# Recurrent-memory attention on one core: V on four column tiles with a bank of late values, Wo kept resident, another stage order

## The chip, the core and the metric

The kernel runs on one core of a Trainium2 chip. A core has TensorE (PE in the profile, with its weight loads as PEld), VectorE (DVE), ScalarE (ACT), GpSimd (POOL) and SyncE (SP, which here only issues transfers). TensorE reads SBUF and writes PSUM; VectorE and ScalarE copy PSUM back to SBUF. PSUM has eight banks, and part B below uses all of them. The metric is device time in microseconds of one execution; lower is better.

## The reference, cut to what matters

Two attentions run side by side and their outputs are concatenated. Part A is a sliding dilated attention, which this change leaves alone. Part B is a segment-recurrent attention with a memory of 8 rows: 64 segments of 32 tokens, model width 640, 32 heads of width 192.

```python
mem = mem0                                    # 8 rows
for s in range(n_seg):                        # 64 segments, in order
    h = jnp.concatenate([mem, xs], axis=1)    # 8 memory rows + 32 tokens = 40
    q = jnp.einsum('btd,dhe->bhte', h, Wq)    # k and v likewise
    scores = jnp.einsum('bhqe,bhke->bhqk', q, k) * scale
    scores = jnp.where(mask[None, None], scores, -1000000000.0)
    p = _softmax(scores, axis=-1)
    o = jnp.einsum('bhqk,bhke->bhqe', p, v)
    o = jnp.einsum('bhte,hed->btd', o, Wo)
    mem = o[:, :M, :].copy()                  # next segment needs this
    outs.append(o[:, M:, :])
```

The first 8 output rows of a segment are the memory of the next one, so the 64 segments form one chain. The four weight matrices of part B are 640 x 6144 each in bf16, too much to keep all of them in SBUF.

## The kernel before

**Order.** Resident weights are loaded first, then part A runs (16 blocks of 128 rows), then part B runs its 64 segments. The order of TensorE's instructions in part B is written out by hand in `segment`; the other engines' orders are laid out by the framework at build, each engine then works strictly in its own order. `evacuate` (line 267) sends PSUM copies to ScalarE and VectorE alternately.

**Rows and tokens.** A segment works on 40 rows: 32 that do not wait for the previous segment's result and 8 that do or nearly do. `HTs` holds the transposed rows in the order memory (8), then the tokens. For Q and K, the pass `project32` takes the first 32 of them (8 memory rows and 24 tokens) as 32-column weights on four column tiles of TensorE, five steps of four matmuls with 384 moving columns each (line 305). The remaining 8 tokens of a segment ("late" rows) are computed for four segments at a time: `XL` holds the late tokens of four segments, `project32` with `XL` fills the banks `Lq` and `Lk`, and GpSimd copies the 8 columns of the current segment from there (line 333). Each Q or K bank is renewed every four segments, so a segment has one doubled K pass and one late Q pass.

**A group of heads.** The 32 heads are worked in four groups of eight. For each group: a Q pass, a K pass, each copied to SBUF (`sb`, line 267) and turned by three matmuls against the identity (`turn`, line 318); the scores (line 368, 16 matmuls); a softmax on VectorE and ScalarE (lines 372 to 382); a V pass over all 40 rows (`values`, line 351, 64-column weights on two column tiles, 20 matmuls); P turned (`turn_p`, line 390, eight transposes); P times V (`mix`, line 404, 24 products over 40 keys in 64x64 tiles, two PSUM tiles, two copies); and the output projection (`project_out`, line 420, 24 matmuls per group) that accumulates into `Y`. At the segment's end `Y` is copied (`Ysb`, line 472), its memory rows are turned by six small matmuls (line 482) into the next `HTs`, and the output rows are stored by GpSimd's queue. `prep` (lines 275 to 284) loads and turns the next segment's tokens.

**Weights.** They are cut into pieces of 128 partitions: Q, K and V pieces of 384 KB and Wo pieces of 480 KB. All Q pieces are resident. `stream_plan` picks which of K, V and Wo are resident as well; the rest, 11 K, 9 V and 5 Wo pieces in each segment (704, 576 and 320 transfers in all), is streamed by SyncE's queue into five buffers at the place of use (`get_unit`, line 237). A buffer's next transfer is issued when TensorE has finished with the piece in it.

**PSUM.** Eight banks: three for the passes (`ps_acc`), two for turns (`ps_tr`), two for scores, turned P and P times V (`ps_at`), one for `Y`. Within a pool the buffers are taken in rotation, and an instruction that takes a buffer waits until the buffer's last reader is done.

Of the kernel before, what the change touches and what calls it, by code (L numbers as in the profile page):

```python
# [152 lines left out]
def stream_plan(budget):  # L153

    k = lambda g: [(("k", g, dc), 0.2) for dc in range(5)]  # L160
    v = lambda g: [(("v", g, dc), 0.35) for dc in range(5)]
    o = lambda g: [(("o", 4 * g + i, 0), 0.44) for i in range(4)]
    gap = lambda t: [(None, t)]
    steps = gap(1.0) + k(0) + gap(1.6) + k(1) + gap(0.8) + v(0) + gap(1.7) + k(2) + gap(0.6) + v(1)
    steps += gap(2.1) + k(3) + gap(0.6) + v(2) + gap(0.7) + o(0) + gap(1.0) + v(3) + gap(0.4)
    steps += o(1) + gap(0.7) + o(2) + o(3) + gap(1.9)
    size = lambda u: 3840 if u[0] == "o" else 3072
    total = sum(size(u) for u, _ in steps if u)
    span = sum(t for _, t in steps)
    for to_stream in range(total - budget, total, 64):  # L170
        now, done, streamed = 0.0, 0, []
        for u, t in steps:
            now += t
            if u is not None and done + size(u) / 2 <= min(5000 + to_stream * now / span, to_stream):
                streamed.append(u)
                done += size(u)
        if total - done <= budget:
            break
    return [u for u, _ in steps if u and u not in streamed]


def part_b(ctx, tc, B_x, B_mem0, B_Wq, B_Wk, B_Wv, B_Wo, out, ident, n_seg, budget, pre, nbuf, mid):
# [7 lines left out]
    wo_v = B_Wo.rearrange("h e d -> (h e) d").rearrange("(i p r) d -> p i (r d)", p=128, r=3)  # L190

    def unit_src(u):
        m, c, dc = u
        if m == "o":
            return wo_v[:, c, :]
        return w_in[m][:, dc, 1536 * c:1536 * c + 1536]
# [4 lines left out]
    resident = [("q", g, dc) for g in range(GROUPS) for dc in range(5)] + stream_plan(budget)  # L201
# [3 lines left out]
    def load_resident(pool, units):  # L205
        for k, u in enumerate(units):
            t = pool.tile([128, unit_cols(u)], BF16, name="wres_%s%d_%d" % u)
            res_engs[k % 2].dma_start(t[:], unit_src(u))
            res[u] = t[:]
# [12 lines left out]
    qk_sb = ctx.enter_context(tc.tile_pool(name="b_qk", bufs=3))  # L222
    one = ctx.enter_context(tc.tile_pool(name="b_one", bufs=1))
    small = ctx.enter_context(tc.tile_pool(name="b_small", bufs=4))
    ps_acc = ctx.enter_context(tc.tile_pool(name="b_ps_acc", bufs=3, space=PSUM))
    ps_tr = ctx.enter_context(tc.tile_pool(name="b_ps_tr", bufs=2, space=PSUM))
    ps_at = ctx.enter_context(tc.tile_pool(name="b_ps_at", bufs=2, space=PSUM))
# [4 lines left out]
    def get_unit(u):  # L232
        if u in res:
            return res[u]
        t = wstream.tile([128, 1920], BF16, tag="ws")
        v = t[:, 0:unit_cols(u)]
        nc.sync.dma_start(v, unit_src(u))
        return v
# [13 lines left out]
    Ps = [cpool.tile([128, 4 * L + PADW], BF16, name=f"P{i}") for i in range(2)]  # L252
# [5 lines left out]
    for t in HTs:  # L258
        nc.gpsimd.memset(t[:], 0.0)
    for t in QTs + Ps + OTs:  # L260
        nc.gpsimd.memset(t[:, t.shape[1] - PADW:], 0.0)
# [7 lines left out]
    def prep(s):  # L269
# [8 lines left out]
        pt = ps_tr.tile([128, 5, L], BF16, tag="tr")  # L278
# [7 lines left out]
    def prep_first():  # L286
# [5 lines left out]
        pt = ps_tr.tile([128, 5, L], BF16, tag="tr")  # L292
# [5 lines left out]
    def project32(Xs, m, g):  # L298

        ps = [ps_acc.tile([128, 384], FP32, tag="acc", name=f"pqk{n}") for n in range(len(Xs))]  # L300
        for dc in range(5):
# [6 lines left out]
        out = []  # L308
        for p in ps:
            sb = qk_sb.tile([128, 384], BF16, tag="sb", name="sb")  # L310
            evacuate(sb[:], p[:])
            out.append(sb)
        return out

    def turn(sb, dst):
        pt = ps_tr.tile([128, 3, 4, 32], FP32, tag="tr")
        for c in range(3):
            nc.tensor.matmul(pt[:, c], lhsT=sb[:, 128 * c:128 * c + 128], rhs=ident, start=True, stop=True)  # L318
        evacuate(dst.rearrange("p (j c) n -> p c j n", c=3), pt[:])
# [4 lines left out]
    def project_qk(s, m, g):  # L324
# [3 lines left out]
        sbs = project32([XL, HTs[s % 2]] if renew else [HTs[s % 2]], m, g)  # L328
# [9 lines left out]
    def project_late(m, g):  # L338
        sb = project32([XL], m, g)[0]
        return lambda: turn(sb, LT[m][g][:])  # L340

    def values(s, g):
        HT = HTs[s % 2]
        Vst = work.tile([128, 2, 384], BF16, tag="Vst")
        pv = [ps_acc.tile([128, 384], FP32, tag="acc", name=f"pv{c}") for c in range(2)]
        for dc in range(5):
            w = get_unit(("v", g, dc))
            for c in range(2):
                for gv in range(2):
                    n = 768 * c + 384 * gv  # L350
                    nc.tensor.matmul(pv[c][64 * gv:64 * gv + 64, :], lhsT=HT[:, dc, :], rhs=w[:, n:n + 384],  # L351
                                     start=(dc == 0), stop=(dc == 4), tile_position=(0, 64 * gv))
        for c in range(2):
            evacuate(Vst[:, c, :], pv[c][:])
        return Vst

    def scores(g):
        QT, KT = QTs[g % 2], tokens(KTs[g % 2])
        Sps = ps_at.tile([128, 4, L], FP32, tag="at")
# [7 lines left out]
        for n, (_, lo, a, g2, cc, hi) in enumerate(plist):  # L367
            nc.tensor.matmul(Sps[64 * g2:64 * g2 + 64, a, :], lhsT=QT[lo:hi, L * cc:L * cc + 64], rhs=KT[lo:hi, cc, :],  # L368
                             start=(g2 not in seen), stop=(n == last[g2]), tile_position=(lo, 64 * g2))
            seen.add(g2)  # L370
        t1 = work.tile([128, 4, L], FP32, tag="t1")
# [10 lines left out]
        nc.vector.tensor_tensor(out=Ps[g % 2][:, 0:4 * L].rearrange("p (a n) -> p a n", n=L), in0=t1[:],  # L382
                                in1=sm[:].unsqueeze(2).to_broadcast([128, 4, L]), op=ALU.mult)

    def turn_p(g):

        pt = ps_at.tile([128, 4, 128], BF16, tag="at")
        for a in range(4):
            for gv in range(2):
                nc.tensor.transpose(pt[64 * gv:64 * gv + 64, a, :], Ps[g % 2][:, L * a:L * a + 64], ident,  # L390
                                    tile_position=(0, 64 * gv))
        PT = work.tile([128, 4, 2, L], BF16, tag="PT")
        evacuate(PT[:], pt[:].rearrange("p a (h n) -> p a h n", h=2)[:, :, :, 0:L])
        return PT

    def mix(g, PT, Vst):

        ps = [ps_at.tile([128, 2, 3, L], FP32, tag="at", name=f"OTps{gv}") for gv in range(2)]
        V = Vst[:].rearrange("p c (h e r) -> p c h r e", h=2, r=3)
        for ai in range(2):  # L400
            for r in range(3):
                for half in range(2):
                    for gv in range(2):
                        nc.tensor.matmul(ps[gv][64 * half:64 * half + 64, ai, r, :],  # L404
                                         lhsT=V[64 * gv:64 * gv + L, ai, half, r, :],
                                         rhs=PT[64 * gv:64 * gv + L, 2 * ai + gv, half, :],
                                         start=True, stop=True, tile_position=(64 * gv, 64 * half))
        dst = OTs[g % 2][:, 0:12 * L].rearrange("p (ai gv n) -> p gv ai n", ai=2, gv=2)
        for gv in range(2):
            evacuate(dst[:, gv], ps[gv][:].rearrange("p a r n -> p a (r n)"))  # L410
# [13 lines left out]
    late = []  # L424

    def segment(s):
# [3 lines left out]
        while late:  # L430
            late.pop(0)()
# [6 lines left out]
        scores(0)  # L438
# [3 lines left out]
        scores(1)  # L442
        tk[2] = project_qk(s, "k", 2)
        tq[2]()
        PT[0] = turn_p(0)
        V[1] = values(s, 1)
        tk[2]()
        mix(0, PT[0], V[0])
        tq[3] = project_qk(s, "q", 3)
        scores(2)  # L450
        tk[3] = project_qk(s, "k", 3)
        tq[3]()
        PT[1] = turn_p(1)
        V[2] = values(s, 2)
        tk[3]()
        mix(1, PT[1], V[1])
        Y = ps_y.tile([128, 320], FP32, tag="y")
        project_out(Y, 0)
        scores(3)
        PT[2] = turn_p(2)  # L460
        if not last:
            prep(s + 1)
        V[3] = values(s, 3)
        mix(2, PT[2], V[2])
        project_out(Y, 1, range(0, 2))
        PT[3] = turn_p(3)
        project_out(Y, 1, range(2, 4))
        mix(3, PT[3], V[3])
        project_out(Y, 2)
        project_out(Y, 3)  # L470
        Ysb = work.tile([128, 320], BF16, tag="Ysb")
        nc.scalar.copy(Ysb[:], Y[:])
        if not last:
            late.append(project_late("q", (s + 1) % 4))
            HTn = HTs[(s + 1) % 2]
            pt = ps_tr.tile([128, 5, M], FP32, tag="tr")
            for dc in range(5):
                for gv in range(2):
                    c0, c1 = max(128 * dc, 320 * gv), min(128 * dc + 128, 320 * gv + 320)
                    if c0 < c1:  # L480
                        lo = c0 - 128 * dc
                        nc.tensor.matmul(pt[lo:lo + c1 - c0, dc, :], lhsT=Ysb[:, c0 - 320 * gv:c1 - 320 * gv],  # L482
                                         rhs=ident[:, 64 * gv:64 * gv + M], start=True, stop=True,
                                         tile_position=(0, lo))
            nc.vector.tensor_copy(HTn[:, :, 0:M], pt[:])  # L485
            late.pop(0)()
# [80 lines left out]
```

## Time and profile before

| | |
|---|---|
| median of 3 runs | 2506.86 us (2502.24 to 2510.97) |
| the profiled execution | 2491.66 us |
| its span | 2489.9 us |
| mean granted TensorE clock | 0.989 |
| first and last copy of Y (64 of them) | 364.0 and 2485.1 us |
| TensorE / VectorE / ScalarE / GpSimd busy | 89% / 49% / 30% / 12% |
| mean DMA rate over the span | 303 GB/s |

All times of the working come from the one profiled execution; it is 0.6% shorter than the median of the timed runs. The span consists of about 320 us of part A with the resident loads and then the 64 segments. In the profile, a row of a group gives line, engine, operation, output and inputs, the count, and the mean time of one instruction; a row in order of time gives start, duration and what ended the idle time before it. Matmuls overlap in TensorE's pipeline, so the durations of single matmuls are latencies, not their share of time: what a stage costs is read from the start of its first instruction to the start of the next stage's first.

### The profile page before, as it was taken

To read this page: it belongs to the slowest core of one execution; us is meant where nothing else is said; L and a number is where in the kernel's file an instruction comes from. 1 tells how busy PE (TensorE), PEld (TensorE's weight loads), DVE (VectorE), ACT (ScalarE), POOL (GpSimd) and SP (SyncE) were. 2 spreads that over 40 slices of the span, in tenths; PEclk is the share of its full clock that TensorE was granted. 3 is DMA by queue.
4 is the path that set the end of the run, shared out by engine and by line. 5 is a ranking of instruction groups with operands and counts; after the bars stand their busy time and mean duration, and the time that the engine had idled before them with its cause. 6 is when DMAs were issued, how large, how long until landed. Compare 5 with 4: busy or idle time off the path is not lost.

```text
span 2489.9 us, 92161 instructions
## 1 busy us (share of the span) xinstructions
PE 2206.2 (89%) x40618; PEld 1473.5 (59%) x40633; DVE 1214.1 (49%) x3110; ACT 749.6 (30%) x1811; POOL 287.7 (12%) x833
## 2 busy tenths in 40 slices
PE   0787679999999999999999999999999999999998
PEld 0455456666666666666665666666666666666665
DVE  1466534454444455444454444455444445444444
ACT  2122223333233333323333333333333333333332
POOL 1011111111111111111111111111011111111100
PEclk9899989999999999999999999999999999999999
DMA  7677689989888898888998899999888989889997
GB/s 294 214 259 255 220 315 320 319 306 311 309 312 315 309 316 307 303 313 303 312 316 298 310 313 311 313 319 318 304 314 315 308 313 312 311 313 316 318 320 270
DMA packets 279344, 754.65 MB, mean 303 GB/s; under 512 B 33192, under 2 KB 60656, under 8 KB 278944
## 3 DMA queue, kind: packets, MB, share of 16 engines
q1 hardware_dynamic: 260656, 705.44, 81.0%
q0 software_dynamic: 14208, 32.59, 4.2%
q10 hardware_dynamic: 4080, 10.73, 1.1%
q8 instruction: 318, 5.21, 0.8%
q14 instruction: 82, 0.67, 0.1%
HBM read 735.49 MB, written 13.15 MB: 301 GB/s over the span
## 4 chain that ended last, share of the span: by engine, by line
PE 48%; DMA 34%; DVE 4%; ACT 2%; issue 1%; ACTq 0%; POOL 0%; SPq 0%; POOLq 0%; DVEq 0%
DMA t<-in_B_Wo_dram 17%; PE pqk L305 16%; PE Y L420 11%; DMA t<-in_B_Wv_dram 10%; PE pv L351 9%; DMA t<-in_B_Wk_dram 6%; PE pt L318 4%; PE Sps L368 3%; PE pt L390 2%; PE OTps L404 2%; ACT sb L267 1%; ACT t L378 1%; DVE t L377 0%; DVE t L372 0%; DVE mx L376 0%
## 5 line engine op out<-in xcount | busy, mean ns | idle before, releaser
L420 PEld LDWEIGHTS <-OT 128*64 128x64 bf16 x6144 | 353.0, 110 | 110.4 <-issue 69.0
L351 PEld LDWEIGHTS <-HT 128*64 128x64 bf16 x5120 | 287.5, 110 | 148.8 <-issue 58.1
L420 PE MATMUL Y<-wres_o,OT 128*64 128x320 bf16 x4224 | 369.1, 301 | 0.0
L305 PEld LDWEIGHTS <-HT 128*32 128x32 bf16 x10240 | 242.5, 96 | 166.5 <-issue 43.2
L351 PE MATMUL pv<-t,HT 128*64 128x384 bf16 x2304 | 284.8, 329 | 40.1 <-DMA t<-in_B_Wv_dram 31.6
L351 PE MATMUL pv<-wres_v,HT 128*64 128x384 bf16 x2816 | 309.0, 328 | 0.2 <-DVE sb L267 0.2
L267 DVE CAST sb<-pqk 128x384 bf16<-128x384 f32 x324 | 180.3, 556 | 238.8 <-PE pqk L305 232.1
L305 PE MATMUL pqk<-wres_q,HT 128*32 128x384 bf16 x5120 | 258.7, 329 | 0.0
L267 ACT CAST sb<-pqk 128x384 bf16<-128x384 f32 x322 | 154.4, 479 | 334.0 <-PE pqk L305 333.3
L420 PE MATMUL Y<-t,OT 128*64 128x320 bf16 x1920 | 188.8, 302 | 54.1 <-DMA t<-in_B_Wo_dram 53.4
L305 PE MATMUL pqk<-t,HT 128*32 128x384 bf16 x2816 | 206.0, 329 | 28.1 <-DMA t<-in_B_Wk_dram 27.7
L318 PE MATMUL pt<-ident,sb 128*128 128x128 bf16 x1938 | 208.4, 222 | 11.6 <-ACT sb L267 11.6
L318 PEld LDWEIGHTS <-sb 128*128 128x128 bf16 x1938 | 109.8, 97 | 171.7 <-issue 111.0
L267 ACT CAST Vst<-pv 128x384 bf16<-128x384 f32 x256 | 122.7, 479 | 288.9 <-PE pv L351 288.2
L267 DVE CAST Vst<-pv 128x384 bf16<-128x384 f32 x256 | 141.5, 553 | 120.7 <-PE pv L351 120.2
L333 POOL COPY QT<-Lq 128x96 bf16<-128x96 bf16 x256 | 69.0, 269 | 917.0 <-PE Sps L368 816.8
L485 DVE CAST HT<-pt 128x40 bf16<-128x40 f32 x63 | 12.6, 200 | 312.3 <-PE pt L482 312.3
L372 DVE SCALAR_TENSOR_TENSOR t<-Sps,mask 128x160 f32<-128x160 f32 x256 | 83.0, 324 | 167.6 <-PE Sps L368 163.2
L305 PE MATMUL pqk<-wres_k,HT 128*32 128x384 bf16 x2304 | 160.4, 327 | 0.0
L368 PEld LDWEIGHTS <-QT 128*64 128x64 bf16 (+1 forms) x4096 | 114.9, 109 | 68.5 <-issue 46.8
L368 PE MATMUL Sps<-KT,QT 128*64 128x40 bf16 (+1 forms) x4096 | 139.0, 188 | 10.3 <-DVE KT L267 9.2
L378 ACT ACTIVATE t<-t 128x160 f32<-128x160 f32 x256 | 86.5, 338 | 203.5 <-DVE t L377 202.4
(93 smaller groups left out, 2570.8 us busy)
## 6 DMA issues: line engine op xcount, KB each, us to landing
t<-in_B_Wk_dram SPq DMA_DIRECT2D x704, 384.0 KB, 4.9
t<-in_B_Wv_dram SPq DMA_DIRECT2D x576, 384.0 KB, 5.1
t<-in_B_Wo_dram SPq DMA_DIRECT2D x320, 480.0 KB, 5.7
K<-a_kv_scr SPq DMA_DIRECT2D x16, 1280.0 KB, 6.2
V<-a_kv_scr POOLq DMA_DIRECT2D x16, 1280.0 KB, 8.8
a_kv_scr<-qkv POOLq DMA_DIRECT2D x16, 320.0 KB, 4.8
wres_q<-in_B_Wq_dram ACTq DMA_DIRECT2D x10, 384.0 KB, 7.8
wres_q<-in_B_Wq_dram SPq DMA_DIRECT2D x10, 384.0 KB, 7.8
```

What stands on the lines that cost most here:

```text
L267: (nc.scalar.copy if copies["n"] % 2 else nc.vector.tensor_copy)(dst, src)
L305: nc.tensor.matmul(ps[n][32 * j:32 * j + 32, :], lhsT=X[:, dc, 0:32], rhs=w[:, 384 * j:384 * j + 384], start=(dc == 0), stop=(dc == 4), ti ...
L318: nc.tensor.matmul(pt[:, c], lhsT=sb[:, 128 * c:128 * c + 128], rhs=ident, start=True, stop=True)
L333: nc.gpsimd.tensor_copy(tokens(T)[:, :, 32:L], LT[m][g][:, :, M * i:M * i + M])
L351: nc.tensor.matmul(pv[c][64 * gv:64 * gv + 64, :], lhsT=HT[:, dc, :], rhs=w[:, n:n + 384], start=(dc == 0), stop=(dc == 4), tile_position= ...
L368: nc.tensor.matmul(Sps[64 * g2:64 * g2 + 64, a, :], lhsT=QT[lo:hi, L * cc:L * cc + 64], rhs=KT[lo:hi, cc, :], start=(g2 not in seen), stop ...
L372: nc.vector.scalar_tensor_tensor(out=t1[:], in0=Sps[:], scalar=scale, in1=mask[:].unsqueeze(1).to_broadcast([128, 4, L]), op0=ALU.mult, op ...
L378: nc.scalar.activation(t1[:], t1[:], ACTF.Exp)
L390: nc.tensor.transpose(pt[64 * gv:64 * gv + 64, a, :], Ps[g % 2][:, L * a:L * a + 64], ident, tile_position=(0, 64 * gv))
L404: nc.tensor.matmul(ps[gv][64 * half:64 * half + 64, ai, r, :], lhsT=V[64 * gv:64 * gv + L, ai, half, r, :], rhs=PT[64 * gv:64 * gv + L, 2 ...
L420: nc.tensor.matmul(Y[64 * gv:64 * gv + 64, :], lhsT=OTs[g % 2][:, L * c:L * c + 64], rhs=w[:, n:n + 320], start=(i == 0 and r == 0), stop= ...
L485: nc.vector.tensor_copy(HTn[:, :, 0:M], pt[:])
```

## The change

The change touches part B alone.

- The V pass takes 32 rows on four column tiles, in the form of the Q and K passes (`project32`). The late rows' values are kept in new banks `LV`, one per group, renewed by a doubled pass (`XL` and `HT`) in one of four segments per group.
- P is written in two parts: 32 columns for the first keys, and 8 columns at the place of the current segment among the 32 late keys, in a tile of 64 columns whose other late columns are zero (GpSimd clears the previous segment's place for groups 0 and 1).
- P is turned by eight transposes with 32 output rows; P times V is a sum over the 32 keys of `Vst` and the 32 late keys of `LV`: 32 products per group, 16 with 128 columns and 16 with 64, on 32-row tiles, into four PSUM tiles with four copies.
- Wo is wholly resident, its rows in another order; 25 pieces of K and V, all of 384 KB, are streamed per segment from a fixed list, into six buffers.
- The two PSUM pools of two banks become one pool of four (`ps_x`). `qk_sb` has two buffers instead of three, `small` two instead of four, `Ysb` one instead of two.
- Stage order: P of a group is turned right after the next group's scores; each group's Wo follows the next group's V; `prep` stands behind the V pass of group 3; the late Q pass is split, three steps ahead of Wo of group 2 and two behind Wo of group 3; Wo of group 2 is split around the last turn and the last product.

```diff
+STREAMED = {"k": ((0, 1, 3, 4), (0, 2), (0, 1), (0, 1, 2, 3)),
+            "v": ((2, 4), (0, 1, 2, 4), (0, 1), (0, 1, 2, 3, 4))}
...
-    wo_v = B_Wo.rearrange("h e d -> (h e) d").rearrange("(i p r) d -> p i (r d)", p=128, r=3)
+    wo_v = B_Wo.rearrange("h e d -> (h e) d").rearrange("(i k p) d -> p i k d", p=128, k=3)
...
-    ps_tr = ctx.enter_context(tc.tile_pool(name="b_ps_tr", bufs=2, space=PSUM))
-    ps_at = ctx.enter_context(tc.tile_pool(name="b_ps_at", bufs=2, space=PSUM))
+    ps_x = ctx.enter_context(tc.tile_pool(name="b_ps_x", bufs=4, space=PSUM))
...
     def values(s, g):
+        renew = s == 0 or s % 4 == (g + 2) % 4
+        ps = project32([XL, HTs[s % 2]] if renew else [HTs[s % 2]], "v", g)
+        if renew:
+            evacuate(LV[g][:], ps[0][:])
+        Vst = work.tile([128, 384], BF16, tag="Vst")
+        evacuate(Vst[:], ps[-1][:])
         return Vst
...
+        i = s % 4
+        P = Ps[g % 2]
+        if g < 2 and s:
+            old = 32 + M * ((s - 1) % 4)
+            nc.gpsimd.memset(P[:, :, old:old + M], 0.0)
...
-        nc.vector.tensor_tensor(out=Ps[g % 2][:, 0:4 * L].rearrange("p (a n) -> p a n", n=L), in0=t1[:],
-                                in1=sm[:].unsqueeze(2).to_broadcast([128, 4, L]), op=ALU.mult)
+        for lo, hi, at in ((0, 32, 0), (32, L, 32 + M * i)):
+            nc.vector.tensor_tensor(out=P[:, :, at:at + hi - lo], in0=t1[:, :, lo:hi],
+                                    in1=sm[:].unsqueeze(2).to_broadcast([128, 4, hi - lo]), op=ALU.mult)
...
     def mix(g, PT, Vst):
+        ps = [ps_x.tile([128, 3, L], FP32, tag="x", name=f"OTps{a}") for a in range(4)]
+        for wide in (True, False):
+            for late, V in enumerate((Vst, LV[g])):
+                for half in range(2):
+                    for a in range(4):
+                        if wide:
+                            dst, e0, e1, col = ps[a][:, 2 * half, :], 256 * half, 256 * half + 128, 0
+                        else:
+                            dst, e0, e1 = ps[a][64 * half:64 * half + 64, 1, :], 128 + 64 * half, 192 + 64 * half
+                            col = 64 * half
+                        nc.tensor.matmul(dst, lhsT=V[32 * a:32 * a + 32, e0:e1], rhs=PT[32 * a:32 * a + 32, late, half, :],
+                                         start=(wide and late == 0 and half == 0), stop=(not wide and late == 1),
+                                         tile_position=(32 * a, col))
+        for a in range(4):
+            evacuate(OTs[g % 2][:, 3 * L * a:3 * L * a + 3 * L], ps[a][:].rearrange("p k n -> p (k n)"))
...
         tq[2] = project_qk(s, "q", 2)
-        scores(1)
+        scores(s, 1)
+        PT[0] = turn_p(0)
         tk[2] = project_qk(s, "k", 2)
         tq[2]()
-        PT[0] = turn_p(0)
+        mix(0, PT[0], V[0])
         V[1] = values(s, 1)
         tk[2]()
-        mix(0, PT[0], V[0])
+        Y = ps_y.tile([128, 320], FP32, tag="y")
+        project_out(Y, 0)
...
+        V[3] = values(s, 3)
         if not last:
             prep(s + 1)
-        V[3] = values(s, 3)
         mix(2, PT[2], V[2])
-        project_out(Y, 1, range(0, 2))
+        if not last:
+            gl = (s + 1) % 4
+            ql = project32([XL], "q", gl, range(0, 3))
+        project_out(Y, 2, range(0, 1))
         PT[3] = turn_p(3)
-        project_out(Y, 1, range(2, 4))
+        project_out(Y, 2, range(1, 3))
         mix(3, PT[3], V[3])
-        project_out(Y, 2)
+        project_out(Y, 2, range(3, 4))
         project_out(Y, 3)
```

## The prediction

> **What bounds the kernel now.** I read first the page's head and busy slices, then the waits, then one segment of part B in order of time, then the windows by stage.
>
> ```profile
> span 2489.9 us, 92161 instructions
> PE 2206.2 (89%) x40618; PEld 1473.5 (59%) x40633; DVE 1214.1 (49%) x3110; ACT 749.6 (30%) x1811; POOL 287.7 (12%) x833
> ...
> L472 ACT CAST Ysb<-Y x64: 426/426/428, 364.0 to 2485.1; 128x320 bf16<-128x320 f32 x64
> ...
> PE Y L420 <- DMA t<-in_B_Wo_dram: 53.4, 71, 2.4
> PE pv L351 <- DMA t<-in_B_Wv_dram: 31.6, 54, 1.1
> PE pqk L305 <- DMA t<-in_B_Wk_dram: 29.2, 51, 1.5
> ...
> 1500.00:1600.00 100.00, 94.02 (x1829) 62.86 (x1827) 49.16 (x138) 31.37 (x79) 11.96 (x36) 1.00 0.92 319
> ```
>
> TensorE is busy nine tenths of the span. One copy of Y ends each of the 64 segments: (2485.1 - 364.0)/63 = 33.67 us per segment is the unit of everything below. The three DMA waits sum to 114 us; with their companions on the weight loads I take 1.9 us per segment. The last row gives 319 GB/s at a DMA share of 0.92, so 347 GB/s would be full use. So the kernel is TensorE in program order, with the stream close behind.
>
> The stretches that carry the sum, TensorE rows first, then the softmax of group 3 and the copies beside it:
>
> ```profile
> 1008.46 1.00 PE L305 MATMUL pqk<-wres_q,HT 128*32 128x384 bf16 x20
> 1009.39 0.51 PE L318 MATMUL pt<-ident,sb 128*128 128x128 bf16 x6
> ...
> 1022.79 0.41 PE L390 MATMUL pt<-ident,P 128*64 128x128 bf16 x8
> 1023.03 0.49 PE L351 MATMUL pv<-wres_v,HT 128*64 128x384 bf16 x4
> ...
> 1024.76 0.34 PE L318 MATMUL pt<-ident,sb 128*128 128x128 bf16 x3
> 1025.03 0.45 PE L404 MATMUL OTps<-PT,Vst 40*64 40x40 bf16 x24
> 1025.41 0.60 PE L420 MATMUL Y<-wres_o,OT 128*64 128x320 bf16 x6
> ...
> 1027.07 0.52 PE L368 MATMUL Sps<-KT,QT 128*64 128x40 bf16 x16
> 1027.52 0.41 PE L390 MATMUL pt<-ident,P 128*64 128x128 bf16 x8
> 1027.64 0.33 DVE L372 SCALAR_TENSOR_TENSOR t<-Sps,mask 128x160 f32<-128x160 f32 x1 [1.60 <-PE Sps L368]
> 1027.87 0.29 PE L280 MATMUL pt<-ident,xr 40*128 40x40 bf16 x5
> 1028.30 0.30 ACT L281 COPY HT<-pt 128x160 bf16<-128x160 bf16 x1
> 1028.63 0.18 DVE L284 COPY XL<-pt 128x40 bf16<-128x40 bf16 x1
> 1029.71 0.32 DVE L382 TENSOR_TENSOR P<-t,sm 128x160 bf16<-128x160 f32 x1
> ```
>
> Matmuls overlap, so I cost TensorE by slots, start to next start. A Q or K pass: 1008.46 to 1009.39, 0.92 us. A V pass: 1023.03 to 1024.76, 1.73 us. Turning P: 0.24 us. P times V: 0.38 us. A softmax needs 1027.07 to 1030.03, 2.96 us from the start of its scores to P written.
>
> **The change, step by step, us per segment (minus is faster).**
>
> *V passes.* Twenty matmuls stay twenty, but on four column tiles instead of two, which is the form of the K pass: 1.73 becomes 0.92, four times: -3.27. The late rows' V is one more such pass inside a doubled one, 20 x 0.041 = +0.82 (the K pass with XL shows this step). All on the path.
>
> *P turned.* Eight transposes with 32 output rows for eight with 64: 0.24 to about 0.20, -0.2 over four groups.
>
> *P times V.* 24 products per group become 32: 16 with 128 columns, then 16 with 64. No row shows 32-row tiles. Lower bound: the old slot scaled, 0.38 x 32/24 = 0.51. Upper: the prep's five products (128-column weights, 40 moving) take 1027.87 to 1028.09, 44 ns each, 32 of them 1.41. I take 0.75: wide ones at the prep's inner pitch (first to last start, about 0.11 us over four steps, overlapped a little), narrow ones at the old 16 ns, and one extra change of tile form at about 0.1 (a pass followed by its like has a slot of 0.82, otherwise 0.92). Four times +0.37: +1.5. The Trainium skill, page "TensorEngine Tiling (Array Packing)", section Key Properties, says that changing the tiling mode drains the engine, which the 0.82 against 0.92 bears out, and it speaks against this mix; with four drains more and nothing else the sum would only move by +0.4.
>
> *Boundary.* Three of five steps of the late Q pass move ahead of Wo and stop covering the copy of Y. From the last Y matmuls (1003.25) to the next segment's first pass took 2.39; Now the memory rows start as soon as Y is copied (1004.32) instead of at 1004.71, which makes it 2.08, and the moved part costs 12 x 0.041 + 0.1 = 0.6 where it now stands: +0.3.
>
> TensorE work in sum: -0.9, bounds -1.9 and +1.8.
>
> *Stream.* 20 pieces of 384 KB and five of 480 KB become 25 of 384 KB: 10.32 to 9.83 MB, at 347 GB/s 29.7 to 28.3 us, with six buffers instead of five. Wo no longer waits. At 1.13 us a piece and six in hand, supply stays ahead of my walk until group 3's five V pieces in a row, where it is short by less than one. DMA waits 1.9 to 0.4: -1.5, bounds -1.9 and 0.
>
> *What is late next.* The two PSUM pools of two banks become one ring of four, and each P times V now takes all four. Its fourth product takes the bank of the turn (groups 0, 1) or of the prep (group 2) issued immediately before it, so TensorE, in order, stands until that copy is out, with the V pass, Wo and everything else queued behind.
> - Groups 0 and 1, at least: a turn's copy starts 0.43 after the turn, takes 0.48 (ScalarE) or 0.55, less the slot of 0.27: 0.7. In the built order the copy stands behind a softmax's exponential or its last write in part of the segments. Group 1: 0.75. Group 0, where the softmax of group 1 is fresh: 1.0.
> - Group 2: the XL copy of the prep, on VectorE, now stands behind the softmax of group 3, since prep moved behind the V pass. From the scores' start TensorE needs 0.48 + 0.20 + 0.92 + 0.22 = 1.82 (2.64 when V is doubled). VectorE needs 2.96, plus 0.2 for a second write of P, 0.2 for a copy of PT in front and 0.2 for XL: 3.6 (4.2 with a V copy between). Wait 1.65.
> - turn of P(0), now right after scores 1, and K of group 1: 0.35. The q3 turn behind the exponential of group 2 on ScalarE: 0.25. First Wo pair after the last mix, 0.15.
>
> Together 4.15. Before, such waits were 0.45 (KT, sb and XL behind VectorE and ScalarE). So +3.7; bounds +1.5 (1.2 instead of 3.4 before the mixes, rival 1) and +5.1 (groups 0 and 1 both at 1.6, behind the last write of P in every segment). The memsets on GpSimd (two per segment) and the token copies behind them are hidden: GpSimd is 12% busy and its longest queue waits for TensorE; without the cover they cost about 0.27 each. The same page, section PSUM Bottleneck, warns that after a fourfold tiling the copies out of PSUM may bind; VectorE at 49% busy would by that rule leave room on average, and it is the order that I charge.
>
> *One-off.* The first segment has four doubled V passes: +3. The Wo rows are read in runs of 1280 bytes instead of 3840, once, 16 pieces: hidden behind segment 0 or up to +10.
>
> **Sum.** -0.9 - 1.5 + 3.7 = +1.3 us per segment, times 63 = +83, plus 3: +86 us. The profiled execution took 2491.66 us (span 2489.9), 15 us under the median 2506.86 of the runs shown. On the median: **2593 us**.
>
> **Rivals.**
> 1. *Faster: the copies come in time.* ScalarE and VectorE lose three of eight V copies per segment (0.48 to 0.55 each), so the queues I see may be shorter, and three of four products start before the held one. With 1.2 us before the mixes instead of 3.4, the sum is -0.9 per segment, -55: 2452 us. It decides where the waits before the three mixes fall below 2.1 us per segment. For it: ScalarE is 30% busy. Against: the order is fixed at build and the softmax chain is longer than the V pass that now covers it.
> 2. *DMA waits stay.* If five V pieces in 0.8 us leave the 1.9 us of waits, +1.5 more: 2688 us. Against: Wo, the largest wait, is resident.
> 3. *P times V at its upper bound* 1.41: +2.6 more, 2759 us. Against: today's mix issues at 16 ns in 64x64 tiles.
> 4. *Nothing changes:* held only by the turn or prep right before (0.7, 0.7, 0.77), the sum is about +0.1: 2510 us.
>
> **How the numbers follow.** Main case 0.50 (own range 2540 to 2645), rival 1 0.24, rival 2 0.10, rival 3 0.10, rival 4 0.06. A change under about 0.3% can't be told from none here. Slower: 0.50 + 0.10 + 0.10 and a part of rival 4 = 0.72; same 0.04; faster 0.24. The range goes from rival 1's value to rival 2's, 2450 to 2690, and leaves out most of rival 3 and the far side of rival 1.
>
> **What would show it.** V slots of 0.92 and a Y period near 35 us; TensorE busy share below 89%; waits of the OTps products on VectorE and ScalarE copies of about 1.0, 0.75 and 1.65 us, the last on XL; DMA waits near 25 us in sum. I am wrong if the OTps products start straight after the turn, or if the mix slot lies far from 0.75.

## The result, and the profile after

The changed kernel takes 2654.60 us (median of 4 runs, 2628.65 to 2659.82) against 2504.55 us (2490.48 to 2510.97) for the kernel before on the same chip: a ratio of 1.0587, interval 1.0503 to 1.067. It is slower by 150 us, 64 more than forecast; the profiled executions, 2659.82 and 2491.66 us, are 168 us apart. In the order of the fences before the prediction:

From the page of the changed kernel (span, busy time, landing of the streamed pieces) and its tile view of Ysb:

```profile
span 2658.0 us, 99823 instructions
PE 2207.7 (83%) x44021; PEld 1331.0 (50%) x44021; DVE 1195.5 (45%) x3527; ACT 713.3 (27%) x1973; POOL 298.8 (11%) x959
...
t<-in_B_Wv_dram SPq DMA_DIRECT2D x832, 384.0 KB, 5.7
t<-in_B_Wk_dram SPq DMA_DIRECT2D x768, 384.0 KB, 5.5
...
L467 ACT CAST Ysb<-Y x64: 425/425/426, 376.3 to 2653.2; 128x320 bf16<-128x320 f32 x64
```

TensorE is busy for the same time as before (2206.2 us then), and the rest of the span has grown. The segment takes (2653.2 - 376.3)/63 = 36.14 us instead of 33.67: 2.47 x 63 = 156 us; the other 12 us lie before the first copy of Y (376.3 instead of 364.0), 3.7 of them in the first segment (44.1 instead of 40.4) and the rest ahead of it, where part B's first pass starts at 332.20 instead of 323.56.

The waits of TensorE in the changed kernel (us in total, times, longest us):

```profile
PE acc L289 <- DMA t<-in_B_Wv_dram: 143.0, 223, 2.2
...
PE OTps L388 <- ACT QT L250: 40.1, 81, 0.8
PE OTps L388 <- DVE XL L267: 36.9, 60, 1.3
PE OTps L388 <- DVE QT L250: 33.2, 46, 1.2
PE acc L289 <- DMA t<-in_B_Wk_dram: 30.2, 55, 1.1
```

The three rows of OTps are the forecast holds of the fourth product: 110 us. The two rows of DMA are not as forecast: 173 us where 25 were expected and where the kernel before had 114.

The timeline of TensorE in one segment of the changed kernel (start, us, operation, count, idle before and its releaser). In order of time: a mix that is held and a V pass; an undisturbed mix of group 3 with the Wo behind it; and, a segment later, the last V pass and the start of the Wo tail:

```profile
1405.39 0.19 PE L388 MATMUL OTps<-PT,Vst 32*128 32x40 bf16 x3
1406.03 0.20 PE L388 MATMUL OTps<-PT,Vst 32*128 32x40 bf16 x5 [0.44 <-ACT QT L250]
...
1406.40 0.71 PE L289 MATMUL acc<-t,HT 128*32 128x384 bf16 x8
...
1407.53 0.34 PE L302 MATMUL pt<-ident,sb 128*128 128x128 bf16 x3
...
1418.35 0.22 PE L388 MATMUL OTps<-PT,Vst 32*128 32x40 bf16 x8
...
1418.74 1.50 PE L402 MATMUL Y<-wres_o,OT 128*64 128x320 bf16 x18
...
1446.81 0.93 PE L289 MATMUL acc<-t,HT 128*32 128x384 bf16 x16
1449.56 0.35 PE L289 MATMUL acc<-t,HT 128*32 128x384 bf16 x4 [1.82 <-DMA t<-in_B_Wv_dram]
...
1451.92 1.01 PE L402 MATMUL Y<-wres_o,OT 128*64 128x320 bf16 x6
1452.86 0.40 PE L370 MATMUL pt<-ident,P 128*32 128x128 bf16 x8
```

Three products of a mix go and the fourth stands until the turn's copy is out (1405.39 to 1406.03). The mix of group 3, with no turn ahead of it, takes 1418.35 to 1418.74, 0.39 us for 32 products. The last V pass stands 1.82 us for its last piece. Six Wo matmuls then take 0.94 us (1451.92 to 1452.86); at the rate of group 0, 24 from 1407.81 to 1409.46, they would take 0.41.

Where the stream is meanwhile: the waits of SyncE's queue (total, times, longest), the DMAs that it issues over the end of this segment, and two windows of the same segment (us, busy time of the five engines, granted clock, DMA share, GB/s):

```profile
SPq L217 <- PE acc L289: 1542.9, 892, 11.4
```

```profile
1440.30 3.79 SPq L217 DMA_DIRECT2D t<-in_B_Wv_dram  x5
1444.19 6.08 SPq L217 DMA_DIRECT2D t<-in_B_Wk_dram  x6
1460.23 1.59 SPq L217 DMA_DIRECT2D t<-in_B_Wv_dram  x2
```

```profile
1426.40:1434.40 8.00, 6.84 (x160) 3.94 (x153) 5.50 (x18) 2.83 (x7) 0.74 (x3) 1.00 1.00 370
...
1454.40:1459.40 5.00, 4.83 (x97) 2.83 (x97) 0.87 (x4) 1.32 (x4) 0.97 (x2) 0.91 0.01 5
```

SyncE issues the next segment's six K pieces by 1450.3, and then nothing for ten microseconds, until TensorE has used the first of them (1459.85). Six pieces are all that six buffers hold. Such waits for a buffer last up to 11.4 us; before, the longest was 3.7. Once these six pieces have landed, the DMA engines do nothing (share 0.01 from 1454.40 to 1459.40); while pieces are being issued they are nearly full (0.91 from 1423.4 to 1450.4, and 1.00 with 370 GB/s in the window shown) and TensorE waits. Before, with five Wo pieces among the 25, five windows of 8 us in a row (1000 to 1040) had shares of 0.75 to 0.99.

Slots on TensorE, start to next start as in the prediction, summed from the traces over 63 segments (us per segment; a wait counts to the slot that it interrupts). The last column is the time between the first and the last copy of Y in which the record of the granted clock stands at one half. The two lower rows are the first two experiments, without streamed transfers:

| | period | Q, K, V passes | Wo | mixes | turning P | half-rate clock in part B, us in all |
|---|---|---|---|---|---|---|
| before | 33.67 | 17.75 | 7.88 | 1.56 | 1.10 | 10 |
| after | 36.14 | 18.04 | 8.12 | 3.94 | 0.70 | 263 |
| b_nostream | 31.22 | 16.47 | 6.78 | 1.53 | 1.06 | 0 |
| a_nostream | 31.50 | 13.95 | 7.13 | 4.54 | 0.61 | 20 |

### The profile page after: what moved, and what is told of

Same layout as the page of the kernel before. It is cut to its first block, busy times and chain, and to the rows that moved or that the text cites. A ratio compares the mean times of both kernels' runs of the same rounds, so it can differ in the third digit from the quotient of the medians.

```text
span 2658.0 us, 99823 instructions
## 1 busy us (share of the span) xinstructions
PE 2207.7 (83%) x44021; PEld 1331.0 (50%) x44021; DVE 1195.5 (45%) x3527; ACT 713.3 (27%) x1973; POOL 298.8 (11%) x959
## 4 chain that ended last, share of the span: by engine, by line
PE 45%; DMA 38%; DVE 7%; ACT 4%; issue 2%; SPq 0%; ACTq 0%; POOL 0%; POOLq 0%; DVEq 0%
DMA t<-in_B_Wv_dram 29%; PE acc L289 18%; PE Y L402 14%; DMA t<-in_B_Wk_dram 5%; PE OTps L388 4%; PE pt L302 3%; DMA K<-a_kv_scr 2%; PE Sps L342 1%; DVE sb L250 1%; DMA a_kv_scr<-qkv 1%; PE pq L65 1%; ACT QT L250 1%; DVE K L98 1%; PE pt L370 1%; ACT sb L250 1%
## 5 line engine op out<-in xcount | busy, mean ns | idle before, releaser
L289 PE MATMUL acc<-t,HT 128*32 128x384 bf16 x6400 | 475.8, 333 | 143.5 <-DMA t<-in_B_Wv_dram 114.4
L289 PEld LDWEIGHTS <-HT 128*32 128x32 bf16 x15360 | 383.8, 97 | 376.7 <-issue 213.9
L402 PE MATMUL Y<-wres_o,OT 128*64 128x320 bf16 x6144 | 552.1, 330 | 1.8 <-issue 1.4
L250 DVE CAST sb<-acc 128x384 bf16<-128x384 f32 x371 | 206.0, 555 | 267.2 <-PE acc L289 222.7
L289 PE MATMUL acc<-wres_q,HT 128*32 128x384 bf16 x5120 | 259.5, 330 | 0.2 <-ACT sb L250 0.2
L388 PE MATMUL OTps<-PT,Vst 32*128 32x40 bf16 (+1 forms) x4096 | 146.9, 197 | 112.8 <-ACT QT L250 40.1
L250 DVE CAST OT<-OTps 128x120 bf16<-128x120 f32 x512 | 121.0, 278 | 229.1 <-PE OTps L388 227.5
L250 ACT CAST sb<-acc 128x384 bf16<-128x384 f32 x275 | 130.8, 476 | 223.8 <-PE acc L289 162.8
L289 PE MATMUL acc<-t,XL 128*32 128x384 bf16 x1676 | 144.1, 337 | 34.7 <-DMA t<-in_B_Wv_dram 28.6
L289 PE MATMUL acc<-wres_k,HT 128*32 128x384 bf16 x2048 | 148.7, 327 | 1.0 <-issue 1.0
```

The lines of the kernel that those rows point to most:

```text
L250: (nc.scalar.copy if copies["n"] % 2 else nc.vector.tensor_copy)(dst, src)
L289: nc.tensor.matmul(ps[n][32 * j:32 * j + 32, :], lhsT=X[:, dc, 0:32], rhs=w[:, 384 * j:384 * j + 384], start=(dc == 0), stop=(dc == 4), ti ...
L388: nc.tensor.matmul(dst, lhsT=V[32 * a:32 * a + 32, e0:e1], rhs=PT[32 * a:32 * a + 32, late, half, :], start=(wide and late == 0 and half = ...
L402: nc.tensor.matmul(Y[64 * gv:64 * gv + 64, :], lhsT=OTs[g % 2][:, L * c:L * c + 64], rhs=w[:, n:n + 320], start=(i == 0 and r == 0), stop= ...
```

## The experiments

Theory S: the 25 pieces are now wanted in the first three quarters of the segment, and what TensorE loses, it loses to the stream. Theory B: the held products (the fourth of each mix) make the loss. Every run is timed against the kernel before on its own chip. That kernel took 2504.55 us on the chip of the result and 2495.41, 2498.12, 2496.99 and 2506.62 us on the four chips below, so a difference in us between runs of two chips is good to about 10 us. All medians:

| run | us | ratio to before |
|---|---|---|
| b_nostream | 2331.52 | 0.9333 [0.928, 0.9387] |
| a_nostream | 2360.38 | 0.9442 [0.9389, 0.9495] |
| a_order | 2599.08 | 1.0403 [1.0328, 1.0479] |
| a_spread | 2581.67 | 1.0343 [1.0272, 1.0414] |
| a_order_nostream | 2175.58 | 0.8711 [0.867, 0.8751] |
| a_both | 2496.28 | 1.0006 [0.9984, 1.0028] |
| a_plan | 2524.52 | 1.0107 [1.0042, 1.0172] |
| a_plan6 | 2367.69 | 0.9492 [0.9444, 0.954] |
| a_spread6 | 2441.10 | 0.9787 [0.9721, 0.9853] |
| b_buf6 | 2390.93 | 0.9571 [0.9512, 0.9629] |
| a_deep7 | 2511.82 | 1.0019 [0.9985, 1.0052] |
| a_deep12 | 2401.86 | 0.9593 [0.9557, 0.9628] |

### Both kernels without streamed transfers

The streamed piece is replaced by a resident one, in the kernel before (b_nostream, where a streamed Wo piece gives way to a resident one of Wo) and in the changed one (a_nostream); this is the edit of the latter:

```diff
-        t = wstream.tile([128, 1536], BF16, tag="ws")
-        nc.sync.dma_start(t[:], unit_src(u))
-        return t[:]
+        return res[("q", u[1], u[2])]
```

> The kernel before, without the streamed transfers: where a K, V or Wo piece would be streamed, a resident Q or Wo piece is read instead, so the output is not the reference's; all matmuls and copies stay. Both theories: the DMA waits of 1.9 us per segment go, 2504 becomes about 2385 us, and the half-rate clock stays rare (10 us before).

> The changed kernel, without the streamed transfers (a resident Q piece is read in place of each of the 25; the output is not the reference's). Theory S (stream: with Wo resident, all 25 pieces are asked for in the first 25 us of a segment, the transfers run full there and idle in the tail; DMA waits of 2.7 us and the half-rate clock behind them are the loss): DMA waits go, 173 us, and the clock recovers, about 95 us: about 2390 us. Theory B (banks: P times V held by the ring of four is the loss): the holds stay and grow from the measured 2.2 to the walked 3.4 us per segment, since nothing else gives the copies time: about 2560 us.

2331.52 and 2360.38 us. So the stream costs 2495 - 2332 = 164 us in the kernel before (2495.41 on this chip) and 2655 - 2360 = 294 us in the changed one (timed on another chip), and all else that the change does costs 29 us. That is S by the forecast. The table of slots shows the 29 us as a difference of larger things: passes 16.47 to 13.95 (-2.52 per segment), mixes 1.53 to 4.54 (+3.01), Wo +0.35, turning P -0.45. The mix slot of group 3 shows that the products themselves cost nothing more, so the +3.01 are holds. From the waits of TensorE in a_nostream:

```profile
PE OTps L386 <- DVE XL L265: 69.3, 60, 1.3
...
PE OTps L386 <- ACT QT L248: 43.5, 81, 0.8
PE OTps L386 <- DVE QT L248: 40.5, 46, 1.2
```

Without DMA waits the holds are longer (153 us against 110), nearly all of it at group 2 (69.3 against 36.9), whose mix stands right behind the V pass of group 3: a wait for a piece of that V gives the copy time to finish.

### The holds taken away, and the stream spread, each alone

a_order moves the mixes of groups 0 and 1 ahead of the turn that they waited for, and the prep ahead of V of group 3; that takes a third buffer for the copies of Q and K, paid for with the second buffer of one scratch tile (these two lines are not shown):

```diff
         tk[2] = project_qk(s, "k", 2)
-        tq[2]()
         mix(0, PT[0], V[0])
         V[1] = values(s, 1)
+        tq[2]()
         tk[2]()
...
-        V[3] = values(s, 3)
         if not last:
             prep(s + 1)
+        V[3] = values(s, 3)
         mix(2, PT[2], V[2])
```

a_spread puts back the old stream, with its five 480 KB buffers (11 pieces of K, 9 of V, 5 of Wo), and leaves the rest of the change:

```diff
-    resident += [(m, g, dc) for g in range(GROUPS) for m in "kv" for dc in range(5) if dc not in STREAMED[m][g]]
-    resident += [("o", i, 0) for i in range(4 * GROUPS)]
+    resident += stream_plan(103700)
...
-    part_b(ctx, tc, B_x, B_mem0, B_Wq, B_Wk, B_Wv, B_Wo, out, ident, n_seg=n_seg, pre=110000, nbuf=6,
+    part_b(ctx, tc, B_x, B_mem0, B_Wq, B_Wk, B_Wv, B_Wo, out, ident, n_seg=n_seg, pre=110000, nbuf=5,
```

> The changed kernel with the holds of P times V taken away by order alone: mix 0 and mix 1 stand before the Q turn instead of behind it, prep before the V pass of group 3; three sb buffers instead of two, t1 single. Theory B: 2.2 us per segment go, about 2515 us. Theory S: the time saved before pieces that are late turns into more DMA waits; only the hold of group 2, behind the last piece, is a gain, 0.9 us per segment: about 2600 us.

> The changed kernel with the stream of before: 11 K, 9 V and 5 Wo pieces in five buffers of 480 KB, the other 15 pieces' worth resident; stage order, banks and V on four tiles as changed. Theory S: demand reaches into the tail again, DMA waits fall from 173 to about 110 us and the clock recovers: about 2500 us. Theory B: holds stay, about 2620 us.

2599.08 and 2581.67 us: 55 and 73 below the changed kernel, neither near a full recovery. In a_order the holds were gone, and TensorE stood for V instead:

```profile
PE acc L289 <- DMA t<-in_B_Wv_dram: 221.1, 333, 3.1
...
PE acc L289 <- DMA t<-in_B_Wk_dram: 17.2, 41, 1.0
```

The DMA waits went from 173 to 238 us. What a hold had cost was mostly time in which the stream caught up. By its number (2600 expected) S is right, but B's cause is there as well, under it.

### The holds without a stream, and both cures together

a_order_nostream is a_order with the edit of a_nostream; a_both is a_order with the edit of a_spread.

> The changed kernel with the holds taken away by order (as in a_order) and without the streamed transfers (a resident Q piece is read instead; the output is not the reference's): what TensorE alone needs. In the changed kernel without transfers a segment took 31.50 us with P times V at 4.54; with P times V at 1.86, as a_order showed it, 28.8 us, 2360 - 170 = 2190 us if the holds are a cost of their own (both theories). If instead the time only moves to other waits of TensorE on the copies, 2280 us or more.

> The changed kernel with the order of a_order and the stream of before (a_spread): holds gone, demand reaching into the tail. Theory S: the two gains do not simply add (-55 and -73 from 2655 would be 2527), because without holds the pieces are wanted even earlier; but the transfers now have the whole segment: 10.3 MB at 347 GB/s is 29.7 us of a 28.8 us walk, so 2450 to 2530 us. Theory B: -2.2 us per segment below a_spread, 2440 us.

2175.58 us: without transfers the holds are worth 2360 - 2176 = 185 us (2.9 per segment), and the changed work without them is 156 us faster than b_nostream. With the old stream back the same order gave 2496.28 us, the time of the kernel before (ratio 1.0006): 85 us below a_spread, but 321 above its own twin without transfers. Without transfers this order saves 31.22 - 28.62 = 2.6 us per segment on the kernel before; with them, five buffers and its stream, it saves nothing (33.59 against 33.67): what TensorE gains it waits for.

### A list by the demand, then a sixth buffer

a_plan is a_both with the streamed pieces spread again by the new order of demand (12 K, 5 V, 8 Wo, 2.9% more bytes); a_plan6 has one buffer more. Its list has as many pieces of each kind, with one Wo piece exchanged for its neighbour:

```diff
-    v = lambda g: [(("v", g, dc), 0.35) for dc in range(5)]
-    o = lambda g: [(("o", 4 * g + i, 0), 0.44) for i in range(4)]
+    v = lambda g: [(("v", g, dc), 0.2) for dc in range(5)]
+    o = lambda a, b: [(("o", i, 0), 0.42) for i in range(a, b)]
...
-    steps = gap(1.0) + k(0) + gap(1.6) + k(1) + gap(0.8) + v(0) + gap(1.7) + k(2) + gap(0.6) + v(1)
-    steps += gap(2.1) + k(3) + gap(0.6) + v(2) + gap(0.7) + o(0) + gap(1.0) + v(3) + gap(0.4)
-    steps += o(1) + gap(0.7) + o(2) + o(3) + gap(1.9)
+    steps = gap(0.8) + k(0) + gap(1.3) + k(1) + gap(0.8) + v(0) + gap(1.7) + k(2) + gap(0.5) + v(1)
+    steps += gap(0.7) + o(0, 4) + gap(1.4) + k(3) + gap(0.5) + v(2) + gap(0.7) + o(4, 8) + gap(0.8) + v(3) + gap(1.1)
+    steps += o(8, 9) + gap(0.2) + o(9, 11) + gap(0.5) + o(11, 16) + gap(1.7)
...
-    resident += stream_plan(103700)
+    resident += stream_plan(102300)
...
-    part_b(ctx, tc, B_x, B_mem0, B_Wq, B_Wk, B_Wv, B_Wo, out, ident, n_seg=n_seg, pre=110000, nbuf=5,
+    part_b(ctx, tc, B_x, B_mem0, B_Wq, B_Wk, B_Wv, B_Wo, out, ident, n_seg=n_seg, pre=110000, nbuf=6,
```

> a_both with the list of streamed pieces laid out anew for this order, evenly over a segment by TensorE's measured stage times: 12 K, 5 V and 8 Wo pieces, five buffers of 480 KB. Theory S: with even demand DMA waits fall below those of before (1.9 us per segment) and the half-rate clock is rare: 2350 to 2420 us, faster than both kernels. Theory B: like a_both.

> a_plan with six buffers of 480 KB instead of five, nearly the same list. If a piece's time to land (5 to 6 us with the queue full) is what the waits come from, 20 to 60 us below a_plan; if the full rate of the transfers is, the same as a_plan.

Two misses. The list by demand made it no better (2524.52 us, 28 above a_both). The buffer, which I had put at 20 to 60 us, was worth 157: 2367.69 us, the fastest kernel here that computes the whole and 5.1% below the one before. The windows of the same 100 us, a_plan and then a_plan6:

```profile
1500.00:1600.00 100.00, 87.67 (x1951) 55.08 (x1948) 46.78 (x157) 29.63 (x85) 12.51 (x42) 0.98 0.94 319
```

```profile
1500.00:1600.00 100.00, 92.11 (x2143) 57.93 (x2137) 49.92 (x170) 31.24 (x92) 13.70 (x46) 1.00 0.98 343
```

The share rose from 0.94 to 0.98 and the bytes per second by 8%, so with five buffers a busy DMA engine moved less as well (319/0.94 = 339 against 343/0.98 = 350 GB/s).

### Which of it is the buffer

a_spread6 is the changed kernel's own order, holds and all, with the stream of a_plan6. b_buf6 is the kernel before with six buffers, and so 26 streamed pieces (11 K, 8 V, 7 Wo), 5.7% more bytes:

```diff
-    part_b(ctx, tc, B_x, B_mem0, B_Wq, B_Wk, B_Wv, B_Wo, out, ident, n_seg=n_seg, budget=103700, pre=110000, nbuf=5,
+    part_b(ctx, tc, B_x, B_mem0, B_Wq, B_Wk, B_Wv, B_Wo, out, ident, n_seg=n_seg, budget=102300, pre=110000, nbuf=6,
```

> The changed kernel, its own stage order with the holds of P times V, but with the stream of a_plan6 (12 K, 5 V, 8 Wo pieces, six buffers of 480 KB). It tells what the holds cost once the stream is mended. If the transfers bind (a_plan6 ran at 345 GB/s in 31.7 us per segment), the holds of 2.2 to 2.85 us fall partly under them: TensorE alone needs 31.5 us here, so about 33 us per segment, 2440 us. If holds and stream add in full: 31.7 + 2.85 = 34.5, 2540 us.

> The kernel before with six buffers of 480 KB instead of five and nothing else but what pays for it: 26 pieces streamed (11 K, 8 V, 7 Wo, 5.7% more bytes). It tells how much of a_plan6 is the sixth buffer. If the sixth buffer does it alone: DMA waits of 1.9 us go, about 2400 us. If five buffers were enough for a TensorE walk of 31.2 us and the bytes count: the same as before or up to 30 us slower.

2441.10 us: with a stream that keeps up the holds are worth 2441 - 2368 = 73 us. Set beside the changed kernel the same run shows what the place of the pieces is worth. Stage order, holds and the number of buffers are the same, and 8% more bytes are moved, but eight pieces are wanted by Wo: the time goes from 2654.60 to 2441.10 us (ratio to before 0.9787 instead of 1.0587, some 200 us), and the DMA waits from 173 to 40 us (22.1 + 10.3 + 8.0).

2390.93 us: the sixth buffer alone makes the kernel before 4.3% faster, against more bytes. So of the gain of a_plan6 over the kernel before (130 us on its chip) 106 come with the buffer, and the changed computation, put in the best order that I found and with 2.7% fewer bytes to move than b_buf6, adds about 1%. Its windows, beside 319 GB/s at a share of 0.92 for the kernel before:

```profile
1500.00:1600.00 100.00, 95.88 (x1909) 63.99 (x1907) 51.83 (x144) 32.29 (x80) 11.70 (x35) 1.00 0.96 345
```

### The changed kernel, only deeper

The stream, the order and the holds as in the changed kernel; the buffers are paid for by leaving pieces of Wo out:

```diff
-    resident += [("o", i, 0) for i in range(4 * GROUPS)]
+    resident += [("o", i, 0) for i in range(11)]
...
+        if u[0] == "o":
+            return res[("o", 0, 0)]
...
-    part_b(ctx, tc, B_x, B_mem0, B_Wq, B_Wk, B_Wv, B_Wo, out, ident, n_seg=n_seg, pre=110000, nbuf=6,
+    part_b(ctx, tc, B_x, B_mem0, B_Wq, B_Wk, B_Wv, B_Wo, out, ident, n_seg=n_seg, pre=110000, nbuf=12,
```

(range(15) and seven buffers in a_deep7)

> The changed kernel with seven streaming buffers instead of six; the last piece of Wo is left out of the chip's memory to make the room (its product reads the first piece instead, so that output columns are summed over a wrong piece of Wo; the work and the 25 streamed pieces stay as they are). Theory D (the stream stops in the Wo tail because its buffers are full): one piece more is fetched in the tail of each segment, so of the demand in the 25 us before it one piece of 384 KB fewer has to come, 1.1 us per segment at the 347 GB/s of full use: 2655 - 70 = about 2585 us, and DMA waits below the 173 us of the changed kernel. Rival (the waits come from how long a piece takes to land under load, not from the buffers): the same within 20 us, 2640 to 2670.

> The same with twelve buffers; the last five pieces of Wo are left out (their products read the first piece). Theory D: the 8.5 us in which the stream stood still are used whole (7.5 pieces at 347 GB/s, of which six more buffers hold six), so DMA waits all but vanish, the half-rate clock with them, and the holds at the products with P remain: between the 2360 us of the changed kernel without transfers and the 2441 us of the spread stream with six buffers, about 2410 us. Rival: 2600 us or more, if the products and waits are bound by the transfers' contention whatever the depth.

2511.82 and 2401.86 us: one buffer more takes back 143 of the 150 us that the change had cost, six take 253. The rival (no effect of depth) falls. The size for twelve was met (2410 expected); for seven it was twice the expected 70. In the profiled execution of a_deep12 the only streamed piece among the longest waits of TensorE in part B is one of 5.6 us, at 338 us, ahead of the first copy of Y; the half-rate clock is down from 263 to 37 us, and the holds stay, as long as without a stream:

```profile
PE OTps L390 <- DVE XL L269: 67.9, 60, 1.8
PE OTps L390 <- ACT QT L252: 43.7, 81, 0.8
PE OTps L390 <- DVE QT L252: 38.9, 46, 1.2
PE acc L291 <- DMA t<-in_B_Wk_dram: 5.6, 1, 5.6
```

The waits of its issue queue on the passes, and the DMA engines in two windows at the end of a segment (the Wo tail is 1432 to 1439 here):

```profile
SPq L219 <- PE acc L291: 1394.9, 855, 9.5
```

```profile
1434.40:1439.40 5.00, 3.12 (x42) 1.85 (x40) 0.70 (x3) 0.85 (x3) 0.00 (x0) 1.00 0.49 181
1439.40:1444.40 5.00, 4.88 (x97) 2.70 (x96) 2.19 (x5) 1.46 (x4) 0.99 (x2) 1.00 0.44 135
```

The issue stands at the end of the segment here too, for ten microseconds (1431.23 to 1441.27): twelve buffers do not keep the stream going where nothing is taken out of them. What they give is a larger stock. The transfers run on into the tail (a share of 0.49 where the changed kernel has 0.01), and the next segment starts with twelve pieces issued instead of six.

Its slots per segment (period 32.00: passes 14.12, Wo 7.33, mixes 4.54) are those of a_nostream within 0.2 each.

## Why the prediction was right, and where it was wrong

The direction held and the time fell into the range, by a sum whose two largest errors had opposite signs, and that is luck. The holds were to make the kernel slower; set against what TensorE gains, they cost 0.3 us per segment when there is no stream. The stream, which was booked as a gain, makes the rest of the loss. Term by term, us per segment:

| term | predicted | measured | from |
|---|---|---|---|
| V passes, late V | -2.45 | -2.8 | passes without the late Q, b_nostream and a_nostream |
| P turned | -0.2 | -0.45 | b_nostream and a_nostream |
| mix, products alone | +1.5 | about 0 | group 3's mix 0.39 against 0.38; a_order_nostream's four 1.57 against 1.53 |
| boundary | +0.3 | +0.2 | late Q +0.27, turns of Ysb -0.09, b_nostream and a_nostream |
| Wo | (0.15, in the next row) | +0.35 | Wo slot, b_nostream and a_nostream |
| holds and other waits | +3.7 | +3.0, as +2.4 in the changed kernel itself | mixes less 1.53 to 1.57 |
| stream | -1.5 | +2.2 | 36.14 - 31.50, less 33.67 - 31.22 |
| one-off, us | +3 | +12 | first copy of Y |

*V passes, boundary: right in kind, each a little better than forecast.* The V pass shown takes 0.60 us for its twelve resident matmuls, the K pass's rate, and 0.53 for the eight streamed ones with the change of tile form ahead of them. From the last Wo matmul to the next segment's first Q pass it takes 1.65 us instead of 2.08 in the pair without transfers, and the twelve matmuls of late Q that moved cost the 0.6 that was forecast.

*The mix: wrong price.* I took 0.75 per mix, between 0.51 and 1.41. The rows show 0.39, below my lower bound: scaling the slot by the count of products was no bound; with twice as many row tiles the products came closer together (12 ns instead of 16). The drain that I charged for one more change of tile form does not show. Rival 3 is out.

*The holds: right mechanism, size a fifth too high.* The fourth product waits, and the row of group 2 names XL, as forecast. Undisturbed (a_nostream) the three sums are 153 us, 2.4 per segment, and 3.0 by slots, against 3.4 forecast. Of the forecast single holds of 1.0, 0.75 and 1.65 us, the last was 69.3/60 = 1.16 on average, and those on the turns' copies 43.5/81 = 0.54 (ScalarE) and 40.5/46 = 0.88 (VectorE). Of the small waits, those at P(0), K1 and the q3 turn (0.60 in sum) do not show: the slots of scores and turns stay within 0.05. That of the first Wo pair (0.15) may be part of the 0.35 by which Wo grew; which part is not shown. Rival 1 (the copies come in time, 2452 us) is out by its time; by its own sign, waits before the mixes below 2.1 us per segment, the changed kernel's rows (110/63 = 1.75) would have spoken for it, and its slots (2.4) against. Rival 4 (whose terms add up to about 2514 us, not 2510) is out by its time too.

*The stream: the step that failed.* "Supply stays ahead of my walk until group 3's five V pieces in a row, where it is short by less than one": I let the supply run on at 347 GB/s through the whole segment and set it against the demand. It can't: with Wo resident nothing is taken out of the buffers in the last ten microseconds, six pieces fill them, and the stream stands. All 25 pieces are then issued in the other 26 us of the segment, with the DMA near its limit (0.88 to 1.00 in windows of 8 to 10 us, at up to 370 GB/s, so 347 was not the most either), and each late piece stops TensorE. Hence DMA waits of 173 us where I wrote 25. My own line "Wo no longer waits" was the gain that I counted; that Wo's five pieces were what kept the stream busy in the tail, I did not see. Rival 2 (DMA waits stay, 2688 us) had the sign, and its ground, five V pieces in 0.8 us, is where the longest wait lies, but the waits did not stay, they grew. a_spread6 shows the cause: with as many buffers and the same order, pieces that are wanted in the tail, in place of some wanted ahead of it, take some 200 us off. a_deep7 and a_deep12 show that a larger stock at the segment's start takes the waits away as well; by themselves they do not tell the tail from any other shortage, since a buffer more also gave 106 us to the kernel before, whose issue waits 3.7 us at the most.

*What I had no term for: the clock.* The granted clock fell from 0.989 to 0.939 and 263 us of part B ran at half rate, in the segment shown behind the last V pass (1451.85 to 1455.26). The Trainium skill, page "TensorE: Matmul & The Clock Gate", section "HAM oscillation — how this bites in real kernels", tells of this: TensorE waits for DMA, its gate falls back to half the clock, and the next work starts slow. The trace agrees with the effect (six Wo matmuls in 0.94 us, 1.82 us lost to a piece just before), but not with that section's measure, gaps of over some 3.4 us: between the first and the last copy of Y no idle gap of TensorE is longer than 2.24 us. The half-rate clock goes when the waits go (20 us in a_nostream, 37 in a_deep12), and a_order, with the most DMA waits, has most of it, 304 us. But the sum of the waits does not decide it: a_plan has 226 us of them and 72 us of half rate. No run held the waits and changed the clock, so how much of the 2.2 us per segment is the clock is not shown. By the slots, Wo, which has no DMA waits, loses 8.12 - 7.13 = 1.0 us per segment against a_nostream, and 1.10 in the kernel before, where its own pieces were waited for.

So: without its stream the change costs 0.3 us per segment where my sum says 2.8, and the stream adds 2.2 where my sum says -1.5. The errors, -2.5 and +3.7, leave +1.2 per segment, 74 us; with 9 more for the one-off that is, but for rounding, the 82 us between +86 and the 168 measured on the profiled executions.

## What to carry to other kernels

Which weights to keep and which to stream is not settled by the bytes: walk the demand through the period, stop the supply where the buffers are full, and look for the stretch in which nothing is streamed; whatever was streamed there kept the pipe going. Here it was worth some 200 us to stream pieces that are wanted there (a_spread6). Before reordering anything, try one buffer more: it was worth 106 to 157 us in three kernels. And where an operation takes a whole ring of PSUM banks, it waits for the copy of the operation issued just before it, so put something else between them, once the stream no longer hides the gain.

## What the runs showed of the hardware

- *The worth of a sixth or seventh buffer.* Five to six: -157 us (a_plan to a_plan6, with the same number of pieces to move) and -106 us (the kernel before to b_buf6, with 5.7% more bytes). Six to seven: -143 us in the changed kernel. A piece lands 5.5 to 5.7 us after its issue and takes 1.13 us of a full stream at 347 GB/s, so about five are under way at full rate, and the one that TensorE reads needs a buffer as well: that is an estimate from these rows, and it fits, but it is only argued. It gives no account of why the seventh, which should give back 1.1 us per segment, gave back 2.3 (143/63). That stays open.
- *Transfers near their limit.* a_plan6 and b_buf6 run at 343 to 345 GB/s with a share of 0.96 to 0.98 over 100 us; over 8 us the changed kernel reached 370 with 1.00. a_order_nostream, the twin of a_plan6 in its order, is 192 us faster without them.
- *Small tiles are cheap.* 32 products on tiles of 32 rows, of 128 and 64 columns, take 0.39 us, 12 ns each.
